# A chunked scan and two mixture layers on one core: the order of the opening, of the weight splits, and of the last columns

## The chip, the cores and the metric

The kernel runs on one core of a Trainium2 chip, in one launch. The metric is the time of one execution on the device in microseconds (us). The core's engines are TensorE (PE in the profile; PEld is its weight load), VectorE (DVE), ScalarE (ACT), GpSimd (POOL) and SyncE (SP), which issues nearly all DMAs.

## The reference

```python
# attention: batch 4, heads 8, seq 768, head_dim 32, state 16
L = np.exp(cum[:, :, :, None] - cum[:, :, None, :]) * causal
M = np.einsum('bhin,bhjn->bhij', Cc, Bc) * L
y = np.einsum('bhij,bhjd->bhid', M, xc) + (C @ state) * np.exp(cum)
state = decay_full * state + sum_j B_j x_j * exp(cum_end - cum_j)
# mixture of 4 experts over 3072 tokens, 256 wide, 1024 hidden
p = domain_probs / (domain_probs.sum(-1, keepdims=True) + 1e-09)
for e in range(E):
    out += p[:, e:e + 1] * (np.maximum(x @ w1[e], 0.0) @ w2[e])
# dense layer, 1536 hidden
return (silu(x @ w_gate) * (x @ w_val)) @ w_out
```

Inputs and output are float32. The chunk length of the scan is the kernel's own choice, as it does not alter what is computed.

## The kernel before

The scan runs in chunks of 128 positions. There are 24 of them, numbered q, 4 batches for each of 6 steps in time. A chunk's y, transposed, is a block of 128 tokens for the first layer. Each 32-bit factor is split into a rounded high part and a low part, and each product of a layer is three products: high by high, low by high, high by low. So weights have to be split too: `w_h` is a copy (ScalarE or POOL), `w_l` a subtraction.

**Opening** (`begin`, line 289, and the code from line 1326). TensorE first runs three products of ones that nothing reads (line 1342), then four mask products (line 198). Once the logarithms of `a` are there (`spaced`, `la`, lines 294 and 295), two prefix products make the cumulated logarithms of chunks 0 and 1 (line 291, `pt` and `py`), VectorE copies them (lines 301 and 302), and 32 small products add them as rows to the masks (`first_rows`, line 205). `first_scores` (line 221) are the products of B and C; ScalarE and VectorE make the decay `L` (lines 239, 248, 253), and `first_weights` (line 257) multiplies scores and decay. `a_heads` (line 546) makes y, `a_done_high` and `a_done_low` (lines 591, 597) split it into `xh` and `xl`, and then the first layer can start. On the way, two products compute the cumulated logarithms of all later chunks and what is left of each chunk (`pc`, lines 308 and 309), two more the rows `crow` that are stored to DRAM (line 334), and read back, spread over the partitions, as `L` of the later chunks (line 419).

**Stream.** From there on the order is written by hand. A unit (e, t, f) is 128 hidden columns f of expert e for token tile t (tiles 0 and 1 have 256 tokens). `m_hidden(u)` (line 662) makes six products into one of three PSUM banks, and ScalarE and VectorE turn them into `hh` and `hl`; `m_out` (line 676) of the unit three before follows. With the last unit of a tile, VectorE multiplies the result by the share of the expert (`tmp`, line 695), and only then may the next tile use the PSUM bank. A unit has two slots; `put(s, fn)` lets `fn` issue its instructions in slot s. What stands in a slot is found in tables: `PAIRS` and `SLOTS` (lines 1370 and 1372) hold the steps of later chunks (per chunk: mask on POOL, exponentials, splits `Cs` and `Bs`, scores; per pair: the slot of its y), and `split_later` (line 1424) the splits of the weights, (e, part), in two pieces each, high and low. `keeps` saves the state after chunks 0 and 1, `blocks_made` makes a block matrix of it on POOL (`bd`), `pair_loads(4)` loads `L` and more for chunks 4 and 5.

**End.** The dense layer uses fewer products by sums of operands. Its last piece, in `plain_product` (line 1254), is made in two halves of 256 columns by `products` (line 990); VectorE adds each half (line 1291), and SP and ScalarE store one each (line 1252).

Of the kernel before, what the change touches and what calls it, by code (L numbers as in the profile page):

```python
# [24 lines left out]
def kernel(ctx: ExitStack, tc: tile.TileContext, nat_d, bc_d, bc0_d, a_d, probs, w1, w2, wg, wv, wo, out):  # L25
# [12 lines left out]
    nc = tc.nc  # L38
    P = 128
# [215 lines left out]
    def first_weights(q, z):  # L255
        L = Q[q]["L"][z]
        nc.vector.tensor_tensor(out=L, in0=first[q][z].rearrange("p (h i) -> p h i", h=4), in1=L, op=ALU.mult)
# [31 lines left out]
    def begin(rows):  # L289

        mm = lambda out, w, v, start=False: nc.tensor.matmul(out, w, v, start=start, stop=True, skip_group_check=True)
        nc.vector.tensor_scalar(out=la, in0=la, scalar1=1e-6, scalar2=1.0, op0=ALU.max, op1=ALU.min)
        n = NFIRST * H
        nc.scalar.activation(out=spaced[:, :, :4], in_=la[:, :n].rearrange("p (g r) -> p g r", r=4), func=AF.Ln)
        nc.scalar.activation(out=la, in_=la, func=AF.Ln)
        nc.scalar.activation(out=wj[:, :1], in_=la[:, :1], func=AF.Exp)
        pt = hidden_bank(512)
        mm(pt[:, :P], spaced.rearrange("p g r -> p (g r)"), upper, True)
        py = ps_s.tile([P, 512], F32, tag="s", name="pc")
        mm(py[:, :n], upper, la[:, :n], True)  # L300
        nc.vector.tensor_copy(sums, pt[:, :P])
        nc.vector.tensor_scalar(out=cum[:, :n], in0=py[:, :n], scalar1=-1.0, scalar2=None, op0=ALU.mult)
        first_rows(rows)
        first_scores(0)
        pr = pt[:GR, P:3 * P]
        for g in range(2):
            mm(pr[:, g * P:(g + 1) * P], la[:, g * GR:(g + 1) * GR], upper)
        mm(py[:, n:NR], upper, la[:, n:])
        mm(py[:, 320:], lower, la)
        high, low = split_parts(0, 0)  # L310
        G = nc.gpsimd
        for z in range(2):
            high(z, G)
            low(z, G)
        first_direct(0, 0, rows[0])
        first_decay(0, 1, rows[1])
        first_decay(1, 0, rows[2])
        first_exp(0, 1)
        first_weights(0, 0)
        first_exp(1, 0)  # L320
        first[1] = out_banks(512)
        first_scores(1)
        mm(pt[:, 3 * P:], ones, ones)
        first_direct(1, 1, rows[3])
        first_weights(0, 1)
        y = ps_y.tile([P, 2, 512], F32, tag="y", name="y01")
        for q in range(2):
            a_place(q, y)
        Q[0]["yv"] = hidden_bank(512)[:, :KD * P].rearrange("p (k i) -> p k i", k=KD)
        Q[0]["y"] = [Q[0]["yv"][:, k, :] for k in range(KD)]  # L330
        a_heads(0, True)
        first_weights(1, 0)
        nc.scalar.activation(out=crow, in_=pr.rearrange("p (g i) -> p g i", g=2), func=AF.Copy)
        nc.sync.dma_start(out=crow_d.rearrange("(g r) i -> r g i", g=2), in_=crow)
        a_load(2)
        expert_load(1, 0, bacc[4])
        a_load_cum(2)
        a_load_nat(2)
        a_load_cum(3)
        a_load_nat(3)  # L340
        first_weights(1, 1)
        a_done_high(0)
        a_done_low(0)
        a_heads(1, True)
        nc.scalar.activation(out=wj, in_=py[:, 320:], func=AF.Exp)
        a_done_high(1)
        a_done_low(1)
        nc.vector.tensor_scalar(out=cum[:, n:], in0=py[:, n:NR], scalar1=-1.0, scalar2=None, op0=ALU.mult)
        high, low = split_parts(0, 1)
        high()  # L350
        for q in range(2):
            a_weigh_b(q, nc.gpsimd)
        low(0, nc.vector)
        return py, lambda: low(1, nc.vector)
# [185 lines left out]
    def a_heads(q, start=False):  # L540
        r = Q[q]
        per = P // D
        for h in range(H):
            j = h % per
            M = r["L"][h // 4][:, h % 4, :] if isinstance(r["L"], list) else r["L"][:, h, :]
            nc.tensor.matmul(  # L546
                r["y"][h // per][j * D:(j + 1) * D, :],
                r["x"][:, h, :],
                M,
                start=(start and h < per),  # L550
                stop=True,
                skip_group_check=True,
            )
# [30 lines left out]
    def a_done_high(q):  # L584
        yv = Q[q]["yv"]
        if q * P >= PLAIN:
            b, o = divmod(q * P, BN)
            nc.scalar.activation(out=bacc[b][:, :, o:o + P], in_=yv, func=AF.Copy)
        else:
            t, o = tile_of(q)  # L590
            nc.scalar.activation(out=xh[t][:, :, o:o + P], in_=yv, func=AF.Copy)
# [395 lines left out]

    retired = []

    def products(ps, w, v, start, stop, parts=1):  # L990
        (wh, wl), (vh, vl) = w, v
        n = BN // parts
        for z in range(0, BN, n):
            for i, (x, y) in enumerate([(wh, vh), (wl, vh), (wh, vl)]):
                nc.tensor.matmul(  # L995
                    ps[:, z:z + n], x, y[:, z:z + n], start=(start and i == 0), stop=(stop and i == 2), skip_group_check=True
                )

    def split(v, engine):
# [250 lines left out]
    def store(src, d, b, z=0, queue=None):  # L1250
        n = src.shape[-1]
        (queue or nc.sync).dma_start(out=out[d * P:(d + 1) * P, b * BN + z:b * BN + z + n], in_=src)

    def plain_product(p, k):

        which, q = divmod(k, NQD)
        tail = p == NPAIR - 1
        V = nc.vector
        fresh = q == 0 and (which != 1 or tail)
        if fresh:  # L1260
            accs[p, which, ""] = bank(*banks[which]) if tail and which else bank(dpools["ps"], "d2")
        elif q == 0:
            accs[p, which, ""] = accs[p, which - 1, ""]
        ps = accs[p, which, ""]
        last = tail and k == 4 * NQD - 1
        parts = 2 if last else 1
        products(ps, wq.pop((p, "plain", k)), sides[p, "plain", k], fresh, q == NQD - 1, parts)
        drop_split(sides.pop((p, "plain", k)))
        if q < NQD - 1:
            return  # L1270
        b1, b2 = 2 * p, 2 * p + 1
        if which == 0:
            c = cs[p] = grab()
            nc.scalar.activation(out=c, in_=ps, func=AF.Copy)
        elif which == 1:
            c = cs[p] if tail else grab()
            if tail:
                chore(9)
                V.tensor_tensor(out=c, in0=ps, in1=c, op=ALU.add)
            else:  # L1280
                nc.scalar.activation(out=c, in_=ps, func=AF.Copy)
            store(c, 1, b1)
            drop(c)
        else:
            if tail:
                chore(9)
            v, d, b = ((ends[p][1], 1, b2), (ends[p][0], 0, b1))[which - 2]
            n = BN // parts
            for i in range(parts):
                f = slice(i * n, (i + 1) * n)  # L1290
                V.tensor_tensor(out=v[:, f], in0=ps[:, f], in1=v[:, f], op=ALU.add)
                store(v[:, f], d, b, i * n, (nc.sync, nc.scalar)[i])
            drop(v)

    order = [(p, k) for p in range(NPAIR) for k in range(4 * NQD)]
# [30 lines left out]
    with tc.manual_schedule():  # L1326
# [11 lines left out]
        constants()  # L1338
        s0 = ps_y.tile([P, 2, 512], F32, tag="y", name="s0")
        first[0] = [s0[:, z] for z in range(2)]  # L1340
        for _ in range(3):
            nc.tensor.matmul(first[0][0][:, :P], ones, ones, start=True, stop=True)
        rows = out_banks(512) + [hidden_bank(512) for _ in range(2)]
        for v in rows:
# [13 lines left out]
        def put(s, *fns):  # L1358
            for fn in fns:
                todo.setdefault(slots[s], []).append(fn)  # L1360
# [5 lines left out]
        def quad(i, j=0, h=0):  # L1366
            return n0 + (i * NQE + j) * 4 + h


        PAIRS = [(0, 0, 28), (0, 0, 46), (0, 0, 60), (6.3, 1.1, 72.5), (6.8, 0.9, 85), (4.3, 1, 95), (4.3, 0.8, 103), (5.8, 1, 117), (5.8, 1.1, 129), (6.8, 1.2, 141), (4.3, 1, 151)]  # L1370

        SLOTS = {
# [6 lines left out]
        }  # L1379

# [57 lines left out]
        put(2, lambda: (mixture(), head_constants()))  # L1438
        put(3, lambda: (mixture_parts(), mixture_store()))
        put(5, lambda: (adds(), loads()))  # L1440
        put(6, keeps)
        put(8, blocks_made)
        put(10, lambda: totals(py[:, 320:]))
        put(14, decays)
        split_later(0, 2, (0, 1), (3, 4))
        split_later(0, 3, (4, 5), (6, 7))
        split_later(1, 0, (6, 9), (10, 13))
        split_later(1, 1, (14, 15), (16, 17), nc.gpsimd)
        split_later(1, 2, (17, 19), (19, 21), nc.gpsimd)
        split_later(1, 3, (26, 27), (28, 29), nc.gpsimd)  # L1450
        put(11, lambda: pair_loads(4))

        seq, t1 = expert_tokens(0, bacc[4], bacc[5])
        for step, slot in zip(seq + [t1], (72, 76, 80, 86, 90, 94, 98, 104), strict=True):
# [304 lines left out]
```

## Time and profile before

| what | value |
|---|---|
| median of 3 runs | 821.24 us (821.04 to 822.31) |
| the profiled execution, own time | 821.02 us |
| its span | 819.3 us |
| PE busy | 811.0 us (99%) |
| DVE, ACT, POOL busy | 563.1, 550.3, 506.2 us |
| DMA | 129.06 MB, mean 158 GB/s |

The span goes from the first to the last instruction that the profiler sees; the time of the execution holds a little more. Busy time is the sum in which an engine has an instruction under way. Where an engine idles, the profile names what ended the idle time: an instruction of another engine, or a DMA. A row of the order of time gives start and duration in us, the engine, the line of the kernel, what is written and read, and how many instructions are merged into the row; in brackets the idle time ahead of it.

### The profile page before, as it was taken

Reading aid. Unit: us, or ns where it says so; the run is one execution under the profiler, and the core shown is the slowest. Engines: PE = TensorE matmul, PEld = TensorE weight load, DVE = VectorE, ACT = ScalarE, POOL = GpSimd, SP = SyncE. Lnnn points to the kernel's source line nnn. Section 1 sums busy time; section 2 is a strip of 40 time slices with the busy share of each in tenths; the row PEclk is TensorE's granted clock in tenths of the full one; section 3 lists DMA queues with packets and bytes.
Section 4 is the critical chain, followed back from the end, with each engine's and each line's share of the span. In section 5 each row is a group of like instructions: output and inputs, shape, how many; then the busy total and the mean of one; then the engine's idle time right before and its main releaser. Section 6 shows DMA issues by size and latency. Waiting matters only on the chain.

```text
span 819.3 us, 12893 instructions
## 1 busy us (share of the span) xinstructions
PE 811.0 (99%) x4361; PEld 671.1 (82%) x4361; DVE 563.1 (69%) x861; ACT 550.3 (67%) x1110; POOL 506.2 (62%) x527
## 2 busy tenths in 40 slices
PE   8999999999999999999999999999999999999998
PEld 7998887888778888888888888887787888888876
DVE  6877567565267855466756565737889878877767
ACT  7687776756476566767766667556577677777763
POOL 5654776434498533777978367313688568847752
PEclk9999999999999999999999999999999999999999
DMA  8864546541302226353552342363556366637651
GB/s 289 281 222 150 162 149 226 172 169 52 116 14 78 90 88 227 97 174 107 164 167 68 121 146 94 138 237 109 174 175 199 129 229 227 227 124 266 228 165 52
DMA packets 67218, 129.06 MB, mean 158 GB/s; under 512 B 6288, under 2 KB 34512, under 8 KB 67152
## 3 DMA queue, kind: packets, MB, share of 16 engines
q1 hardware_dynamic: 67008, 128.11, 47.2%
q8 instruction: 34, 0.56, 0.3%
q14 instruction: 32, 0.26, 0.1%
q10 hardware_dynamic: 144, 0.13, 0.0%
HBM read 108.41 MB, written 19.81 MB: 157 GB/s over the span
## 4 chain that ended last, share of the span: by engine, by line
PE 93%; POOL 2%; ACT 2%; DVE 1%; issue 1%; DMA 1%; DVEq 0%; POOLq 0%; ACTq 0%; SPq 0%
PE h L968 32%; PE d L1088 11%; PE po L1088 10%; PE h L631 10%; PE po L639 9%; PE d L968 7%; PE d L995 6%; PE o L995 3%; PE ypsum L546 1%; PE h L995 1%; PE scores L475 1%; PE ypsum L491 1%; DMA L<-crow_d 1%; POOL acc L872 0%; POOL xl L715 0%
## 5 line engine op out<-in xcount | busy, mean ns | idle before, releaser
L1053 DVE TENSOR_TENSOR d<-d,c 128x512 f32<-128x512 f32 x32 | 22.4, 699 | 103.1 <-ACT c L1050 103.1
L673 DVE SCALAR_TENSOR_TENSOR hl<-h,hh 128x512 fp32r<-128x512 f32 (+1 forms) x80 | 46.5, 582 | 59.7 <-ACT hh L672 59.4
L1088 PE MATMUL d<-hh,we_o 128*128 128x512 f32 x256 | 78.8, 389 | 0.0
L1088 PE MATMUL po<-hh,we_o 128*128 128x512 f32 x256 | 78.8, 389 | 0.0
L1037 DVE SCALAR_TENSOR_TENSOR hl<-h,hh 128x512 fp32r<-128x512 f32 x96 | 65.9, 688 | 17.9 <-PE d L1088 12.9
L672 ACT ACTIVATE hh<-h 128x512 fp32r<-128x512 f32 (+1 forms) x80 | 40.5, 509 | 53.8 <-PE h L631 52.8
L1036 ACT ACTIVATE hh<-h 128x512 fp32r<-128x512 f32 x96 | 57.0, 597 | 26.3 <-DVE h L1057 22.8
L433 ACT ACTIVATE L<-L,cum 128x128 f32<-128x128 f32 x176 | 56.1, 394 | 1.7 <-POOL L L426 1.7
L631 PE MATMUL h<-xh,w_h 128*128 128x512 f32 (+1 forms) x160 | 56.5, 354 | 0.7 <-POOL Bw L461 0.7
L968 PE MATMUL h<-xh,wq_h 128*128 128x512 f32 x144 | 56.5, 392 | 0.4 <-DVE ds L1139 0.3
L639 PE MATMUL po<-hh,w_h 128*128 128x512 f32 (+1 forms) x160 | 56.3, 352 | 0.6 <-DVE tmp L695 0.6
L1088 PEld LDWEIGHTS d<-hh,we_o 128*128 128x128 f32 x256 | 48.1, 188 | 10.0
L1088 PEld LDWEIGHTS po<-hh,we_o 128*128 128x128 f32 x256 | 48.0, 188 | 10.0
L968 PE MATMUL h<-xh,wq_l 128*128 128x512 f32 x144 | 56.1, 390 | 0.0
L968 PE MATMUL h<-xl,wq_h 128*128 128x512 f32 x144 | 56.1, 390 | 0.0
L631 PE MATMUL h<-xh,w_l 128*128 128x512 f32 (+1 forms) x160 | 55.8, 349 | 0.0
L639 PE MATMUL po<-hh,w_l 128*128 128x512 f32 (+1 forms) x160 | 55.6, 347 | 0.0
L639 PE MATMUL po<-hl,w_h 128*128 128x512 f32 (+1 forms) x160 | 55.5, 347 | 0.0
L631 PE MATMUL h<-xl,w_h 128*128 128x512 f32 (+1 forms) x160 | 55.3, 347 | 0.0
L968 PE MATMUL h<-xh,we_h 128*128 128x512 f32 x128 | 50.0, 391 | 0.1
L968 PE MATMUL h<-xl,we_h 128*128 128x512 f32 x128 | 49.8, 389 | 0.0
L968 PE MATMUL h<-xh,we_l 128*128 128x512 f32 x128 | 49.8, 389 | 0.0
(492 smaller groups left out, 2539.4 us busy)
## 6 DMA issues: line engine op xcount, KB each, us to landing
wq_h<-wd_d SPq DMA_DIRECT2D x36, 448.0 KB
wq_l<-wd_d SPq DMA_DIRECT2D x36, 448.0 KB
L<-crow_d SPq DMA_DIRECT2D x22, 512.0 KB
bc<-in_bc_dram SPq DMA_DIRECT2D x21, 512.0 KB
wq_o<-wp_d SPq DMA_DIRECT2D x24, 384.0 KB
raw_q<-in_w_dram SPq DMA_DIRECT2D x32, 256.0 KB
wq_s<-ws_d SPq DMA_DIRECT2D x18, 384.0 KB
pbc<-probs_d SPq DMA_DIRECT2D x22, 256.0 KB
```

The costliest lines, as they stand in the source:

```text
L433: nc.scalar.activation(out=L[:, h, :], in_=L[:, h, :], func=AF.Exp, bias=cols(cum, q)[:, h:h + 1])
L475: nc.tensor.matmul(ps[:, 2 * g:2 * g + 2, :], r["Bs"][:, 2 * half + g, :], r["Cs"][:, 2 * half + g], start=(g == 0), stop=True, skip_group ...
L631: nc.tensor.matmul(ps, w[:, k, fs], v[:, k, :], start=(i == 0), stop=(i == len(ops) - 1))
L639: nc.tensor.matmul(po[d], w[:, fc, dsl], x, start=(first and i == 0), stop=(last and i == 2))
L672: nc.scalar.activation(out=hh, in_=ph, func=AF.Relu)
L673: nc.vector.scalar_tensor_tensor(out=hl, in0=ph, scalar=0.0, in1=hh.bitcast(F32), op0=ALU.max, op1=ALU.subtract)
L968: nc.tensor.matmul(ps, x[:, ws], y, start=(start and i == 0), stop=(i == 2), skip_group_check=True)
L995: nc.tensor.matmul(ps[:, z:z + n], x, y[:, z:z + n], start=(start and i == 0), stop=(stop and i == 2), skip_group_check=True)
L1036: S.activation(out=hh, in_=ps, func=AF.Relu)
L1037: return lambda: V.scalar_tensor_tensor(out=hl, in0=ps, scalar=0.0, in1=hh.bitcast(F32), op0=ALU.max, op1=ALU.subtract)
L1053: V.tensor_tensor(out=W, in0=W, in1=v, op=ALU.add)
L1088: nc.tensor.matmul(po[d], both[:, z, dsl], y, start=(first and i == 0), stop=(last and i == 2), skip_group_check=True)
```

## The change

Of the three products of ones, one stays ahead of the masks and one goes behind the prefix products; the third product of ones, later in `begin`, is dropped. The two products for the later chunks are written behind y of chunk 0. The second half of chunk 1's weights and `xh` of chunk 0 come ahead of `crow`. In the tables, chunk 5's steps come two slots earlier, one step of chunks 2 and 7 moves by a slot, the pair 4 and 5 by one; the pieces of the weight splits are spaced anew, and the high part of expert 1's first weights is made on POOL in place of ScalarE. The last columns are made, added and stored in pieces of 256, 128 and 128.

```diff
@@ begin
         mm(py[:, :n], upper, la[:, :n], True)
+        mm(first[0][0][:, :P], ones, ones, True)
         nc.vector.tensor_copy(sums, pt[:, :P])
...
             mm(pr[:, g * P:(g + 1) * P], la[:, g * GR:(g + 1) * GR], upper)
-        mm(py[:, n:NR], upper, la[:, n:])
-        mm(py[:, 320:], lower, la)
         high, low = split_parts(0, 0)
...
         first_scores(1)
-        mm(pt[:, 3 * P:], ones, ones)
         first_direct(1, 1, rows[3])
...
         a_heads(0, True)
+        mm(py[:, n:NR], upper, la[:, n:])
+        mm(py[:, 320:], lower, la)
         first_weights(1, 0)
+        first_weights(1, 1)
+        a_done_high(0)
         nc.scalar.activation(out=crow, in_=pr.rearrange("p (g i) -> p g i", g=2), func=AF.Copy)
...
         a_load_nat(3)
-        first_weights(1, 1)
-        a_done_high(0)
         a_done_low(0)
@@ products
-    def products(ps, w, v, start, stop, parts=1):
+    def products(ps, w, v, start, stop, edges=(0, BN)):
         (wh, wl), (vh, vl) = w, v
-        n = BN // parts
-        for z in range(0, BN, n):
+        for z, end in zip(edges, edges[1:]):
             for i, (x, y) in enumerate([(wh, vh), (wl, vh), (wh, vl)]):
                 nc.tensor.matmul(
-                    ps[:, z:z + n], x, y[:, z:z + n], start=(start and i == 0), stop=(stop and i == 2), skip_group_check=True
+                    ps[:, z:end], x, y[:, z:end], start=(start and i == 0), stop=(stop and i == 2), skip_group_check=True
                 )
@@ plain_product
-        parts = 2 if last else 1
-        products(ps, wq.pop((p, "plain", k)), sides[p, "plain", k], fresh, q == NQD - 1, parts)
+        edges = (0, BN // 2, 3 * BN // 4, BN) if last else (0, BN)
+        products(ps, wq.pop((p, "plain", k)), sides[p, "plain", k], fresh, q == NQD - 1, edges)
...
-            n = BN // parts
-            for i in range(parts):
-                f = slice(i * n, (i + 1) * n)
+            for i, (z, end) in enumerate(zip(edges, edges[1:])):
+                f = slice(z, end)
                 V.tensor_tensor(out=v[:, f], in0=ps[:, f], in1=v[:, f], op=ALU.add)
-                store(v[:, f], d, b, i * n, (nc.sync, nc.scalar)[i])
+                store(v[:, f], d, b, z, (nc.sync, nc.scalar)[i % 2])
@@ the opening and the tables
-        for _ in range(3):
+        for _ in range(1):
             nc.tensor.matmul(first[0][0][:, :P], ones, ones, start=True, stop=True)
...
-        PAIRS = [(0, 0, 28), (0, 0, 46), (0, 0, 60),
+        PAIRS = [(0, 0, 28), (0, 0, 47), (0, 0, 60),
...
-            5: (31, 33, 34, 34, 36, 40, 45),
+            5: (29, 31, 32, 32, 36, 38, 43),
             6: (37, 39, 40, 42, 43, 47, 50),
-            7: (44, 46, 47, 48, 50, 54, 57),
-            2: (8, 10, 11, 12, 13, 14, 10),
+            7: (44, 46, 46, 48, 50, 54, 57),
+            2: (8, 10, 11, 12, 14, 14, 10),
...
-        put(6, keeps)
+        put(7, keeps)
...
-        split_later(0, 2, (0, 1), (3, 4))
+        split_later(0, 2, (1, 2), (1, 2))
         split_later(0, 3, (4, 5), (6, 7))
-        split_later(1, 0, (6, 9), (10, 13))
-        split_later(1, 1, (14, 15), (16, 17), nc.gpsimd)
+        split_later(1, 0, (6, 9), (10, 13), nc.gpsimd)
+        split_later(1, 1, (13, 15), (15, 16), nc.gpsimd)
...
-        put(11, lambda: pair_loads(4))
+        put(10, lambda: pair_loads(4))
```

Three places show what moves. The first is TensorE in the opening, from the products for the rows `crow` (`upper,la`) to y of chunk 1; `s`, `po` and `h` are PSUM tiles, `pc` is `py`. Before:

```order
L291 MATMUL h_179<-upper,la 96x128 x2
L291 MATMUL pc<-la,upper 128x176
L291 MATMUL pc<-la,lower 128x192
L221 MATMUL po_228<-acc_88 128x128
...
L221 MATMUL po_229<-acc_88 128x128
L291 MATMUL h_179<-ones 128x128
L546 MATMUL h_245<-L,nat 32x128 x8
L546 MATMUL y_244<-L,nat 32x128 x8
```

With the change:

```order
L291 MATMUL h_177<-upper,la 96x128 x2
L221 MATMUL po_225<-acc_88 128x128
...
L221 MATMUL po_226<-acc_88 128x128
L546 MATMUL h_241<-L,nat 32x128 x8
L291 MATMUL pc<-la,upper 128x176
L291 MATMUL pc<-la,lower 128x192
L546 MATMUL y_240<-L,nat 32x128 x8
```

The scores of chunk 1 and y of chunk 0 (line 546, first row) now come right behind the `crow` products, and the `pc` products lie between the two chunks' y; the product of ones is gone.

The second is POOL early in the stream, from the shares `pn` to the first `Bw` of a later chunk. `acc_90` and `acc_91` hold the raw weights of expert 1, parts 0 and 1; line 271 is the high part, line 426 the mask of a chunk. Before:

```order
L370 TENSOR_TENSOR pn<-pin,psm 128x96
L426 AFFINE_SELECT L<-L 128x1024
L577 TENSOR_TENSOR bd<-pairblk,st 128x128 x2
L426 AFFINE_SELECT L<-L 128x1024
L461 TENSOR_TENSOR Bw<-nat,wj 128x128
L271 CAST w_1_0_h<-acc_91 128x512 x2
```

With the change:

```order
L370 TENSOR_TENSOR pn<-pin,psm 128x96
L271 CAST w_1_0_h<-acc_90 128x512
L426 AFFINE_SELECT L<-L 128x1024
L577 TENSOR_TENSOR bd<-pairblk,st 128x128 x2
L271 CAST w_1_0_h<-acc_90 128x512
L426 AFFINE_SELECT L<-L 128x1024
L271 CAST w_1_0_h<-acc_91 128x512
L461 TENSOR_TENSOR Bw<-nat,wj 128x128
```

Two casts are new on this queue, one ahead of the first mask and one behind the blocks.

The third is VectorE at the end of tile 0, where `tmp` (line 695) frees the PSUM bank; the numbers tell the `h` banks apart. Before:

```order
L673 SCALAR_TENSOR_TENSOR hl<-h_791,hh 128x256
L453 SCALAR_TENSOR_TENSOR Cs<-bc,csel,Cs 128x4x128 x2
L484 TENSOR_TENSOR L<-scores,L 128x512
L673 SCALAR_TENSOR_TENSOR hl<-h_821,hh 128x256
L695 TENSOR_TENSOR tmp<-po_609,pbc 128x256
```

With the change:

```order
L453 SCALAR_TENSOR_TENSOR Cs<-bc,csel,Cs 128x4x128 x2
L673 SCALAR_TENSOR_TENSOR hl<-h_798,hh 128x256
L484 TENSOR_TENSOR L<-scores,L 128x512
L673 SCALAR_TENSOR_TENSOR hl<-h_819,hh 128x256
L695 TENSOR_TENSOR tmp<-po_607,pbc 128x256
```

The two `Cs` pieces of chunk 5 now stand ahead of one more `hl`, so one unit earlier.

## Rows read from the trace of the kernel before

**Rows 1.** The page: busy us, share and count of TensorE; granted clock in 40 slices.
```profile
PE 811.0 (99%) x4361; PEld 671.1 (82%) x4361; DVE 563.1 (69%) x861; ACT 550.3 (67%) x1110; POOL 506.2 (62%) x527
PEclk9999999999999999999999999999999999999999
```

**Rows 2.** Waits of TensorE: for whom, us in total, times, longest.
```profile
PE h L631 <- POOL Bw L461: 0.7, 1, 0.7
PE po L639 <- DVE tmp L695: 0.6, 1, 0.6
```

**Rows 3.** Order of time, TensorE, the opening: start, duration, instruction, idle time before.
```profile
1.10 1.65 PE L1342 MATMUL s<-ones 128*128 128x128 f32 x6 [1.10 <-DVE ones L127]
2.54 1.06 PE L198 MATMUL po<-above,upto 128*128 128x512 bf16 x2
...
4.25 0.56 PE L291 MATMUL h<-upper,spaced 128*128 128x128 f32 x2
...
5.29 0.38 PE L205 MATMUL po<-sums,pick 32*128 32x128 f32 x2 [0.35 <-DVE cum L302]
...
7.79 0.46 PE L291 MATMUL pc<-la,upper 128*128 128x176 f32 x2
...
8.51 1.16 PE L221 MATMUL po<-acc 16*128 16x128 f32 x16
9.60 0.49 PE L291 MATMUL h<-ones 128*128 128x128 f32 x2
10.01 0.64 PE L546 MATMUL h<-L,nat 128*32 128x128 f32 x16
...
11.11 0.43 PE L546 MATMUL y<-L,nat 128*32 128x128 f32 x8 [0.17 <-DVE L L257]
12.21 0.36 PE L631 MATMUL h<-xh,w_h 128*128 128x256 f32 x1 [0.67 <-POOL Bw L461]
```

**Rows 4.** Order of time, ScalarE, the opening.
```profile
3.12 0.22 ACT L294 ACTIVATE spaced<-la 128x16 f32<-128x16 f32 x1 [1.05 <-DVE la L292]
...
8.51 1.16 ACT L253 ACTIVATE L<-h,cum 128x128 f32<-128x128 f32 x4
10.12 0.38 ACT L333 ACTIVATE crow<-h 96x256 f32<-96x256 f32 x1 [0.45 <-PE h L291]
```

**Rows 5.** Order of time, VectorE, the opening and the end of tile 0.
```profile
7.70 1.28 DVE L257 TENSOR_TENSOR L<-s,L 128x512 f32<-128x512 f32 x2
9.77 1.29 DVE L257 TENSOR_TENSOR L<-po,L 128x512 f32<-128x512 f32 x2 [0.79 <-PE po L221]
...
41.34 1.41 DVE L453 SCALAR_TENSOR_TENSOR Cs<-bc,csel,Cs 128x512 fp32r<-128x512 f32 x2
...
43.60 0.75 DVE L695 TENSOR_TENSOR tmp<-po,pbc 128x256 f32<-128x256 f32 x2
```

**Rows 6.** Order of time, POOL, from the opening to 26 us.
```profile
9.38 1.28 POOL L275 TENSOR_TENSOR w_l<-raw,w_h 128x512 fp32r<-128x512 f32 x1
...
18.15 1.63 POOL L426 TENSOR_SCALAR_AFFINE_SELECT L<-L 128x1024 f32<-128x1024 f32 x1 [1.76 <-DMA L<-crow_d]
19.75 0.88 POOL L577 TENSOR_TENSOR bd<-pairblk,st 128x128 f32<-128x128 f32 x2
...
23.10 2.54 POOL L271 CAST w_h<-acc 128x512 fp32r<-128x512 f32 x4 [0.35 <-DMA acc<-in_w_dram]
```

**Rows 7.** Order of time, TensorE and its weight load, in the stream.
```profile
17.08 0.19 PEld L631 LDWEIGHTS h<-xh,w_l 128*128 128x128 f32 x1 [0.23 <-DVE w_l L275]
...
23.73 0.28 PE L631 MATMUL h<-xh,w_h 128*128 128x256 f32 x1
...
44.16 0.36 PE L639 MATMUL po<-hh,w_h 128*128 128x256 f32 x1 [0.55 <-DVE tmp L695]
```

**Rows 8.** Order of time, the last products and adds.
```profile
814.67 0.87 PE L995 MATMUL d<-t24l,wq_o 128*128 128x256 f32 x6
815.58 0.76 DVE L1291 TENSOR_TENSOR acc<-d,acc 128x256 f32<-128x256 f32 x2 [0.70 <-PE d L995]
```

More of the change, by code (lines that the diff above doesn't have):

```diff
@@ L1367, in quad @@
             return n0 + (i * NQE + j) * 4 + h
-        PAIRS = [(0, 0, 28), (0, 0, 46), (0, 0, 60), (6.3, 1.1, 72.5), (6.8, 0.9, 85), (4.3, 1, 95), (4.3, 0.8, 103), (5.8, 1, 117), (5.8, 1.1, 129), (6.8, 1.2, 141), (4.3, 1, 151)]
+        PAIRS = [(0, 0, 28), (0, 0, 47), (0, 0, 60), (6.3, 1.1, 72.5), (6.8, 0.9, 85), (4.3, 1, 95), (4.3, 0.8, 103), (5.8, 1, 117), (5.8, 1.1, 129), (6.8, 1.2, 141), (4.3, 1, 151)]
         SLOTS = {
             4: (22, 24, 25, 26, 28, 29, 35),
[1 row of a table removed]
[1 row of a table added]
             6: (37, 39, 40, 42, 43, 47, 50),
[2 rows of a table removed]
[2 rows of a table added]
             3: (13, 15, 16, 17, 18, 22, 22),
```

## The prediction

> **What bounds the kernel now.** I read the page first, then the waits of TensorE, then its order of time in three stretches, and last the order of time of the other engines just ahead of each wait. The page shows TensorE busy for 811.0 of 819.3 us [rows 1], so there are 8.3 us in which it does not work, and only changes to those, or to products that it need not do in their place, can move the end. The waits of TensorE [rows 2] name the two longest that this change is near: 0.7 us ahead of the first product of the first layer, put down to Bw, and 0.6 us on tmp. The third thing to see is that "busy" hides something in the opening: up to 12.21 us [rows 3] TensorE does small products whose only purpose is to let the first layer start, so their order counts, busy or not. From 12.21 us on the products follow each other closely, and what the stream gains at its start it keeps, unless some other engine or a DMA cannot follow.
>
> Times are against the profiled execution: span 819.3, its own time 821.02, which is 0.22 under the median of the three runs, 821.24.
>
> **Fillers ahead.** Three of them run from 1.10 to the masks at 2.54, so 0.48 each [rows 3]. The four masks take 1.71 (2.54 to 4.25), 0.43 for 512 columns, which is the 1.2 GHz level. With two fillers gone the masks could end at 3.29 instead of 4.25, but the prefix product behind them loads spaced, which ScalarE writes from 3.12 to 3.34 [rows 4], and the load of it (an estimate of 0.2 or 0.3, from the 0.40 that the product's two passes take) comes first. I take 3.6, so 0.65 earlier. **Filler behind.** TensorE idles 0.35 ahead of the row products at 5.29 [rows 3]; the filler lies in that hole, moved to 4.29 to 4.64. At 0.48 it sticks out by 0.13, at the higher clock by nothing. The row products therefore start 0.6 earlier, with 0.3 (spaced's load slower, filler all cold) and 0.75 as the ends.
>
> **Order behind the row products.** Two things leave the path of the first chunk's y: the later totals' products (7.79 to 8.51, 0.72) and the last product of ones (9.60 to 10.01, 0.41) [rows 3]. That last one also writes the PSUM tile from which ScalarE copies crow, and crow starts at 10.12, behind it [rows 4], with xh of the first chunk queued behind crow. In the new order:
> - scores of chunk 1 start at 8.51 - 0.72 - 0.6 = 7.19 and take 1.09, to 8.28;
> - VectorE's weights of chunk 0 end at 8.98 [rows 5], now 8.38, so y of chunk 0 starts at 8.4 instead of 10.01 and ends near 8.9;
> - the totals' 0.72 follow, to about 9.65, beside VectorE's weights of chunk 1, which cover them;
> - those weights have two releasers. Half 0 needs the scores (8.28) and VectorE free (8.38): 8.4 to 9.0. Half 1 needs ScalarE's direct exponentials, which end at 8.51 + 1.16 = 9.67 [rows 4], now 9.07: with half of the 1.29 [rows 5] it ends at 9.75;
> - the second half of chunk 1's y starts 0.05 behind that, as before (11.06 and 11.11): 9.8. That is 1.3 earlier.
>
> From there to the first layer it is y, ScalarE's xh, the first load: 12.21 - 1.3 = 10.9. Crow, wj and xh of chunk 0 fit on ScalarE before that, since crow no longer waits for the ones. If the totals' products were late, wj would be late and with it Bw on POOL; but nothing in the stream reads Bw for three units. POOL's low half of the first weights ends at 9.38 + 1.28 = 10.66 [rows 6] and does not move with any of this; the fourth product of the layer reads it, some 0.4 behind the first. So the gain here is 1.3, with 0.7 (no gain from the fillers at all) and 1.45 as ends, and POOL would stop it soon after.
>
> **Respaced splits.** The low half of the weights of part 2 holds TensorE at 17.08 for 0.23 [rows 7]. Its VectorE pieces move from slots 3 and 4 to 1 and 2, ahead of one hl and of the reciprocal, and ScalarE's copies alternate with hh: I take 0.2, and hl and the reciprocal that now stand behind them have over a unit to spare. **Chunk 5's steps** move two slots earlier. At 44.16 TensorE waits 0.55 for tmp [rows 7]; VectorE starts tmp at 43.60 with no idle time ahead of it [rows 5], so it was late through its own queue, in which the two Cs pieces (1.41 from 41.34) stand a few instructions ahead. With these gone from there tmp starts when the products allow, and hl of the unit before is then the last thing ahead of it: 0.5, with 0.3 and 0.55 as ends. Pair 4 and 5 a slot later, keeps a slot later and the L loads a slot earlier cost nothing that I can find: y of that pair is read from slot 64 on, the blocks of keeps first in that pair, and SP issues its DMAs in the same order as before, with one store more at the end.
>
> **POOL gets two casts** of expert 1's first weights, from ScalarE: about 0.64 each by the 2.54 for four [rows 6]. The first falls in the 1.76 idle ahead of the mask at 18.15 and costs nothing; the second stands behind that mask and the blocks. That is the weak place, see the third rival.
>
> **Last columns.** VectorE's first add starts at 815.58, when all six products have ended (814.67 + 0.87 = 815.54), not the first three [rows 8]; its order shows one wait for all pieces, before and after. So three pieces do not let the adds start earlier. The products become three of 256 and six of 128 columns: 0 to 0.36 longer (half the time each, or the same); I take 0.1, near the lower end, since 16 score products of 128 columns take 1.09. The adds take 0.1 more than the 0.76. Against that the last piece to be stored is 64 KB and not 128. Its store is issued some 0.2 later, on SP, behind SP's first, and moves in less: 0, between a loss and a gain of 0.2.
>
> **Sum:** 1.3 + 0.2 + 0.5 + 0 = 2.0, so 819.0 for such an execution and 819.2 for the median.
>
> **The clock.** The masks run at the 1.2 GHz level and the last products, six of 256 columns in 0.87, at 2.4 [rows 3, 8], while the page's granted clock shows 9 in every slice [rows 1]: the change of level is too early for it. TensorE was working from 1.10 until then almost without a hole. The new order keeps that: one filler, masks, prefix, a filler, rows. The Trainium skill (TensorE: Matmul & The Clock Gate, What's actually happening) says that the throttled state is the default and that activity releases it; by that rule fewer fillers speak against this change, and it is the second rival. The trace agrees that the opening starts low; no row here shows a hole that delays the release.
>
> **Rivals.**
> 1. *The stream starts earlier, but waits later for what DMAs bring.* POOL waits for DMAs at 18.15 and at 23.10 [rows 6]; those landings hardly move, since crow, which starts the first of them, is a copy of only 0.8 earlier and its queue is full. Behind 23.10 stand four casts (2.54), VectorE's low halves, and hl in VectorE's order. For: these copies are now a slot or two earlier in VectorE's queue, so hl waits behind them. Against: hl lags its reader by three units. If it takes 1.2 of the 1.3: 820.4. Chance 0.22.
> 2. *The clock rises later.* Products between 5.29 and 8.0 (2.7 us) would take twice that. The gain of 1.3 turns into a loss of 1.4; the other terms (0.7) stay: 821.9. Chance 0.08.
> 3. *Slower: the second cast on POOL.* The layer's first unit of expert 1 starts at 23.73 [rows 7], at 22.2 in the new order, and its second half reads the low piece about 0.5 later, 22.7. On POOL that cast is queued behind the mask (1.63), which waits for L's DMA, and the blocks (0.88) [rows 6]: with the landing at 18.15 the cast ends at 21.3, and VectorE's low piece near 22. It decides from a landing of 18.9 on, and each us more is one us of wait. Slower than now by over 0.2% needs a landing at about 22.5: 823 and more. Against: crow is issued earlier, not later. Chance 0.05.
> 4. *The change does not do what it says in the opening:* spaced or the filler gives the two fillers' time back. Then 0.7 + 0.2 + 0.5 (ends as above): 819.8. Chance 0.10.
>
> **How the numbers follow.** Forecast 0.55: 819.2, by its ends 818.6 to 819.7. 0.2% of 821.24 is 1.64, about what a measurement of this kernel can tell from no change, so faster means under 819.6, slower over 822.9. Nearly all of the forecast (0.53), a third of rival 4 and a little of rival 1 are faster: 0.58. Rival 3 and the tail of rival 2 are slower: 0.06. The rest is 0.36. The range reaches up to rival 1 and past it a little, 820.9, and down to 818.4, where all terms are at their good ends.
>
> **What would show it.** Right: first product of the layer near 10.9 (12.21 before); y of chunk 0 ahead of the totals' products, near 8.4; no waits at the places of 17.08 and 44.16; first mask near 1.6 to 1.75; TensorE's idle time near 7; the last add still behind the last product. Wrong: the first row product later than 5.0, a new wait of TensorE on w_l or hl between 20 and 35 us, or a first layer at 10.9 with the same end, which would put the loss behind 45 us, where I see no cause.

## The result, and the profile after

The changed kernel takes **825.82 us** (median of 6, 823.95 to 826.33) against 821.17 for the kernel before (6 runs, 821.04 to 822.34): a ratio of 1.0051, 95% interval 1.0041 to 1.0061. It is slower by 4.65 us where 2.0 of gain were forecast. The profiled execution took 826.33, with a span of 824.6, 5.3 more than before.

The page first, busy time and granted clock, as in [rows 1]:

```profile
PE 817.5 (99%) x4360; PEld 676.5 (82%) x4360; DVE 567.5 (69%) x862; ACT 549.2 (67%) x1108; POOL 506.9 (61%) x529
PEclk9999999999999999999999999999999999999999
```

TensorE has one instruction less and is busy 6.5 us longer. So the time did not go into a wait. Its waits, as in [rows 2], say the same:

```profile
PE h L631 <- ACT xh L591: 0.7, 1, 0.7
PE ypsum L546 <- ACT L L433: 0.3, 1, 0.3
PE po L639 <- ACT ec L468: 0.2, 1, 0.2
```

The 0.6 on tmp is gone. The wait of the first layer is as long as before and now put down to xh. The order of time on TensorE shows where the 5.3 us are (start, duration, instruction, idle time before; compare [rows 3]):

```profile
1.10 0.80 PE L1340 MATMUL s<-ones 128*128 128x128 f32 x2 [1.10 <-DVE ones L127]
1.72 1.03 PE L198 MATMUL po<-above,upto 128*128 128x512 bf16 x2
...
3.49 0.77 PE L291 MATMUL h<-upper,spaced 128*128 128x128 f32 x2
4.05 0.45 PE L291 MATMUL pc<-la,upper 128*128 128x16 f32 x2
4.34 0.77 PE L291 MATMUL s<-ones 128*128 128x128 f32 x2
5.04 0.58 PE L205 MATMUL po<-sums,pick 32*128 32x128 f32 x2
...
6.91 1.92 PE L221 MATMUL s<-acc 16*128 16x128 f32 x16
8.76 1.17 PE L291 MATMUL h<-upper,la 128*96 128x128 f32 x4
9.86 2.08 PE L221 MATMUL po<-acc 16*128 16x128 f32 x16
11.86 1.08 PE L546 MATMUL h<-L,nat 128*32 128x128 f32 x16
...
16.16 0.55 PE L631 MATMUL h<-xh,w_h 128*128 128x256 f32 x1 [0.67 <-ACT xh L591]
...
19.71 0.41 PE L631 MATMUL h<-xh,w_l 128*128 128x256 f32 x1
19.92 0.41 PE L631 MATMUL h<-xl,w_h 128*128 128x256 f32 x1
...
21.18 0.28 PE L631 MATMUL h<-xh,w_l 128*128 128x256 f32 x1
21.30 0.28 PE L631 MATMUL h<-xl,w_h 128*128 128x256 f32 x1
```

The row products start at 5.04, 0.25 before [rows 3]. From there on the same products take 1.7 to 1.8 times as long: 16 score products 2.08 instead of 1.16, 16 products of y 1.08 instead of 0.64. The products of the first layer, 256 columns, start 0.21 apart at 19.71 and 0.12 apart at 21.18. So TensorE leaves the 1.2 GHz level at about **21.1 us**; the trace's clock record has the change at 21.09, and at 4.61 in the kernel before. TensorE was at work without a hole from 1.10 to beyond 15 us. The page's clock row shows 9 in the first slice of 20.6 us all the same: the trace's record has no entry ahead of this change, and that time is shown as full clock. So the level of so short a stretch is to be read from the spacing of the products.

The first layer starts 3.95 later than before, and by the end of the stretch at the low level the stream is 6.1 behind. At the places of the respaced splits and of chunk 5's steps it wins back 0.3 and 0.4 (5.8 behind, then 5.4). Most of the other 0.4 comes past 700 us: there the kernel before waits 0.3 for `ds` (line 1139), and the changed kernel does not. The end, as in [rows 8]:

```profile
819.72 1.14 PE L994 MATMUL d<-t24l,wq_o 128*128 128x256 f32 x9
820.89 0.82 DVE L1289 TENSOR_TENSOR acc<-d,acc 128x256 f32<-128x256 f32 x3 [0.96 <-PE d L994]
```

The last group starts 5.05 later than in [rows 8], and the span ends 5.3 later: the tail costs 0.25.

### The profile page after: what moved, and what is told of

It reads as the page before. It is cut to its first block, busy times and chain, and to the rows that moved or that the text cites. A ratio compares the mean times of both kernels' runs of the same rounds, so it can differ in the third digit from the quotient of the medians.

```text
span 824.6 us, 12898 instructions
## 1 busy us (share of the span) xinstructions
PE 817.5 (99%) x4360; PEld 676.5 (82%) x4360; DVE 567.5 (69%) x862; ACT 549.2 (67%) x1108; POOL 506.9 (61%) x529
## 4 chain that ended last, share of the span: by engine, by line
PE 93%; POOL 2%; ACT 2%; DMA 1%; issue 1%; DVE 0%; SPq 0%; DVEq 0%; POOLq 0%; ACTq 0%
PE h L968 32%; PE d L1087 11%; PE po L1087 10%; PE h L631 9%; PE po L639 8%; PE d L968 7%; PE d L994 6%; PE o L994 3%; DMA L<-crow_d 1%; PE h L994 1%; PE ypsum L546 1%; PE scores L475 1%; PE ypsum L491 1%; POOL acc L872 0%; POOL xl L715 0%
## 5 line engine op out<-in xcount | busy, mean ns | idle before, releaser
L1087 PE MATMUL d<-hl,we_o 128*128 128x512 f32 x128 | 49.8, 389 | 0.0
```

Of the source, the lines that this page charges most:

```text
L1087: nc.tensor.matmul(po[d], both[:, z, dsl], y, start=(first and i == 0), stop=(last and i == 2), skip_group_check=True)
```

## The experiments

**Theory A:** the loss is the later rise of TensorE's clock, and the two products of ones taken from the start are what brought it about. **Rivals:** the new order of the opening loses time of itself; the tables make new waits in the stream. The first four kernels take the change apart. In the diffs, "ahead" is the loop of products of ones in front of the masks, "behind" the one after the prefix product. The kernel before has three ahead, none behind and one more later in `begin`, so four in all; the changed kernel has two.

**1. The changed kernel, three ahead.**

```diff
-        for _ in range(1):
+        for _ in range(3):
             nc.tensor.matmul(first[0][0][:, :P], ones, ones, start=True, stop=True)
```

> The changed kernel with three products of ones ahead of the masks again, and the one behind the prefix products kept. Clock theory (the two products taken away ahead of the masks leave TensorE at its 1.2 GHz level until 21 us): the level rises before 6 us as in the kernel before, the first product of the first layer comes near 11.3, and the time is 819 to 820.5. Order theory (the new order behind the row products costs the time by itself, the low level only goes with it): the first layer stays behind 15 us and the time over 823.

Measured: 820.67 (819.32 to 822.43, 11 runs), ratio 0.9992 (0.9982 to 1.0001). The clock rises at 5.23, the first layer starts at 11.88 (11.3 was expected), and the loss is gone, with a median just over the expected range. All the rest of the change is in this kernel, so the rest is not the loss.

**2. The kernel before, with the fillers of the change alone.**

```diff
         mm(py[:, :n], upper, la[:, :n], True)
+        mm(first[0][0][:, :P], ones, ones, True)
...
-        for _ in range(3):
+        for _ in range(1):
```

> The kernel before with one edit of the change alone: one product of ones ahead of the masks in place of three, and one behind the prefix products. Clock theory: the products of the first layer start at 0.21 us spacing and the time is 825 to 828, 4 to 7 over the kernel before. Order theory: the time is 820.5 to 821.5.

Measured: 826.07, but in **two groups**: 819.77, 820.3, 820.38 and 820.75, and seven from 826.04 to 826.89; nothing between. Ratio 1.0038 (1.0016 to 1.006). The profiled execution was one of the lower group, 820.3. Its opening:

```profile
1.10 0.80 PE L1343 MATMUL s<-ones 128*128 128x128 f32 x2 [1.10 <-DVE ones L127]
1.72 1.03 PE L198 MATMUL po<-above,upto 128*128 128x512 bf16 x2
...
4.22 0.77 PE L291 MATMUL s<-ones 128*128 128x128 f32 x2
...
8.23 1.16 PE L221 MATMUL po<-acc 16*128 16x128 f32 x16
...
11.94 0.36 PE L632 MATMUL h<-xh,w_h 128*128 128x256 f32 x1 [0.67 <-POOL Bw L462]
12.13 0.28 PE L632 MATMUL h<-xh,w_l 128*128 128x256 f32 x1
12.25 0.28 PE L632 MATMUL h<-xh,w_h 128*128 128x256 f32 x1
```

Here the clock rose at 5.15. So the fillers alone bring the loss, but not in each execution.

**3. The kernel before, with the tables alone** (chunk steps, pairs, keeps, splits, L loads).

```diff
-            5: (31, 33, 34, 34, 36, 40, 45),
+            5: (29, 31, 32, 32, 36, 38, 43),
...
-        split_later(0, 2, (0, 1), (3, 4))
+        split_later(0, 2, (1, 2), (1, 2))
```

> The kernel before with the tables of the change alone (chunk steps, respaced splits, casts on POOL, keeps and loads by a slot). By the prediction's terms 0.2 and 0.5: no wait at 17.08, most of that at 44.16 gone, time 820.3 to 820.7. If the waits are only replaced by others behind them: 821.0 to 821.4.

Measured: 821.21 (820.38 to 822.55, 11 runs), ratio 1.0000 (0.9991 to 1.0008). In its profile, the waits of TensorE:

```profile
PE h L631 <- POOL Bw L461: 0.7, 1, 0.7
PE ypsum L546 <- ACT L L433: 0.4, 1, 0.4
PE po L205 <- DVE cum L302: 0.2, 1, 0.2
PE po L639 <- ACT ec L468: 0.2, 1, 0.2
```

The 0.6 on tmp is gone, and so is the wait at 17.08. From the first product of the first layer to the end of the span it takes 806.38, against 807.09 before: 0.71 less. The median lies where the rival (waits only replaced) was expected, but it can't settle this, at an interval of some 0.7 us to either side; the gain is read from one profile.

**4. The kernel before, with the order of the opening alone** (three ahead, none behind).

```diff
-        mm(py[:, n:NR], upper, la[:, n:])
-        mm(py[:, 320:], lower, la)
...
-        mm(pt[:, 3 * P:], ones, ones)
...
         a_heads(0, True)
+        mm(py[:, n:NR], upper, la[:, n:])
+        mm(py[:, 320:], lower, la)
...
```

> The kernel before with the order of the change behind the row products alone (totals' products between the two chunks' y, second weights and xh ahead of crow, last product of ones dropped), three products of ones ahead as before. By the prediction's working without its filler term: the first layer starts 0.7 us earlier, near 11.5, and the time is 820.3 to 820.7. If the order itself costs, as by the order theory: over 822.

Measured: 820.73 (819.81 to 822.34, 11 runs), ratio 0.9994 (0.9985 to 1.0002); first layer at 11.89. Its opening behind the row products:

```profile
7.48 0.68 PE L291 MATMUL h<-upper,la 128*96 128x128 f32 x4
8.09 1.16 PE L221 MATMUL po<-acc 16*128 16x128 f32 x16
9.18 0.65 PE L545 MATMUL h<-L,nat 128*32 128x128 f32 x16
9.76 0.56 PE L291 MATMUL pc<-la,upper 128*128 128x176 f32 x2
10.16 0.49 PE L291 MATMUL pc<-la,lower 128*128 128x192 f32 x2
10.57 0.65 PE L545 MATMUL y<-L,nat 128*32 128x128 f32 x16
```

y of chunk 1 (10.57) starts when the totals' products end, with no idle time ahead of it. The rivals fall: neither the order nor the tables lose time.

The next four ask how many products of ones it takes, and where.

**5. The changed kernel, two ahead, one behind** (`range(2)` in the loop ahead).

> The changed kernel with two products of ones ahead of the masks where it has one; the one behind the prefix product stays. Theory A (what costs the time is that TensorE goes from 1.2 to 2.4 GHz at 21.09 us and not near 5 us, and what decides is how much TensorE works ahead of about 5 us): with one of the two fillers given back part of the executions, or all, have the early rise; those lie at 819.5 to 822.5, the others near 826, and nothing lies between 823 and 825. Theory B (all three fillers ahead are needed): all executions near 825.8. Theory C (the later rise is an accident of one execution and the lost time lies in the order): near 825.8 too, but with an early rise in the profile.

Measured: 820.85 (819.11 to 822.12), all 11 below 823; ratio 0.9992 (0.9983 to 1.0). One more filler is enough in these executions; theories B and C fall.

**6. The changed kernel, one ahead, three behind.**

```diff
-        mm(first[0][0][:, :P], ones, ones, True)
+        for _ in range(3):
+            mm(first[0][0][:, :P], ones, ones, True)
```

> The changed kernel with one product of ones ahead of the masks, and three instead of one behind the prefix product: as many as in the run with three ahead, two of them 2 us later. The row products then start near 6.0 us (5.04 in the changed kernel, 0.48 for each of two more). Theory A (the amount of work ahead of about 5 us decides, not where it stands): the two more come only between 4.3 and 5.8 us; if that still counts, all executions lie at 820 to 823, with the rise near 6; if it does not, most near 826.5, with the rise near 21. Theory B (the place counts, an unbroken start from 1.10 us): near 826.5 in all.

Measured: 821.52 (819.19 to 826.24, 12 runs), nine of them at most 822.41 and three at 824.84, 826.15 and 826.24; ratio 1.0011 (0.9995 to 1.0028). So fillers that come only at 4.3 us still make the early rise more frequent (nine of 12; without a filler behind two of 12, in run 7; with one behind nine of 30, by the table below), but not sure. The profiled execution, 819.19, has the earliest rise of all, 4.37, and the row products at 5.18 and not near 6.0:

```profile
4.32 0.93 PE L291 MATMUL s<-ones 128*128 128x128 f32 x6
5.18 0.38 PE L205 MATMUL po<-sums,pick 32*128 32x128 f32 x2
...
8.86 0.64 PE L547 MATMUL h<-L,nat 128*32 128x128 f32 x16
...
11.57 0.36 PE L632 MATMUL h<-xh,w_h 128*128 128x256 f32 x1 [0.67 <-ACT xh L592]
```

**7. The changed kernel, one ahead, none behind.**

```diff
-        mm(first[0][0][:, :P], ones, ones, True)
```

> The changed kernel without the product of ones behind the prefix product, and with one ahead. Theory A (the amount of TensorE's work in the opening decides when 2.4 GHz comes): even fewer executions with the early rise than in the changed kernel, so none of 11: all at 824 to 827, rise near 21 us in the profile. Rival (the filler behind is what delays the rise, by holding up the row products): the early rise comes back, 820 to 822.

Measured: 825.2 (819.61 to 826.14, 12 runs); two at 819.61 and 820.1, ten from 823.89 up; ratio 1.0036 (1.0021 to 1.0051). The profile (826.14) has the rise at 21.19. "None of 11" was too strict. Two of 12 and nine of 30 are too few to tell one filler behind from none; but the filler behind is not what delays the rise.

**8. Three ahead, none behind, two pieces at the end** (the rest as changed).

> A version meant to beat both: the changed kernel with three products of ones ahead as before the change and none behind, and with the kernel before's last columns in two pieces. By the terms read so far: early rise in all executions, the order of the opening 0.3 to 0.4 us, the slots of the splits 0.7, no loss of 0.25 in the tail: 820.2 in the median against 821.2, lowest near 819.2. If the order and the slots do not add up, 820.7.

Measured: 820.94 (820.26 to 821.86, 11 runs), ratio 0.9993 (0.9984 to 1.0001): 0.7 more than expected, though all lie below 823. The profiled execution, 821.86, has the rise at 6.59 and a wait that the profiles of runs 1 to 7 do not have. TensorE, POOL, ScalarE and VectorE, one after the other:

```profile
25.65 0.39 PE L630 MATMUL h<-xh,w_l 128*128 128x256 f32 x1 [1.21 <-DVE w_l L275]
```

```profile
21.50 1.10 POOL L425 TENSOR_SCALAR_AFFINE_SELECT L<-L 128x1024 f32<-128x1024 f32 x1 [3.27 <-DVE w_l L275]
...
23.39 0.61 POOL L271 CAST w_h<-acc 128x512 fp32r<-128x512 f32 x1
```

```profile
22.64 1.28 ACT L432 ACTIVATE L<-L,cum 128x128 f32<-128x128 f32 x4 [3.37 <-POOL L L425]
23.83 0.36 ACT L671 ACTIVATE hh<-h 128x256 fp32r<-128x256 f32 x1
```

```profile
24.22 0.42 DVE L672 SCALAR_TENSOR_TENSOR hl<-h,hh 128x256 fp32r<-128x256 f32 x1 [2.78 <-ACT hh L671]
24.56 1.03 DVE L275 TENSOR_TENSOR w_l<-acc,w_h 128x512 fp32r<-128x512 f32 x1
```

The mask starts at 21.50 instead of 18.15 [rows 6], and TensorE waits 1.21 for VectorE's low piece (24.56). That is the late mask of the third rival, but its second cast is not the last link: it ends at 24.00. What holds the low piece until 24.56 is hl ahead of it in VectorE's queue; hl waits for ScalarE's hh, and hh stands behind exponentials that wait for the mask. The mask itself waits for L: VectorE's w_l, which the row names, is no input of it, and in run 11, with the same wait, the row names L's DMA. That load is issued at 13.77 in run 11 and at 14.05 in run 5, whose mask starts at 18.19; why it lands later isn't known, nor how many of the executions have this wait.

**9. The changed kernel again**, unaltered.

> The changed kernel, unaltered, in more executions. Theory A (the rise of TensorE's clock comes by chance early or late, and the less TensorE does before 5 us the rarer it is early): most of the executions at 824 to 827, with at most 4 of 11 at 819 to 822. Rival (the changed kernel always has the late rise): all at 823.9 to 826.5.

Measured: 824.45 (818.84 to 826.03, 12 runs), ratio 1.0019 (0.9999 to 1.0038). Five lie at 818.84, 818.96, 819.69, 821.12 and 821.78, seven from 823.93 to 826.03. So the changed kernel has the early rise too, in some executions; one more than the bound of four that was set. The profiled one (825.23) rises at 20.26.

**10. The kernel of run 2 again**, for a second profile.

> The kernel before with only the fillers moved, unaltered, for a second profile. Theory A: if this execution takes about 826, its clock rises near 21 us and its first layer starts near 16; if it takes about 820, the rise is near 5 us and the first layer near 11.9, as in the first profile. Rival (the two groups differ in something other than the clock, a DMA for one): a time of 826 with a first layer near 12 and the loss later.

Measured: 826.52, rise at 20.85. Its opening, line for line beside that of run 2:

```profile
1.10 0.79 PE L1343 MATMUL s<-ones 128*128 128x128 f32 x2 [1.10 <-DVE ones L127]
1.72 1.03 PE L198 MATMUL po<-above,upto 128*128 128x512 bf16 x2
...
4.17 0.77 PE L291 MATMUL s<-ones 128*128 128x128 f32 x2
...
10.91 2.08 PE L221 MATMUL po<-acc 16*128 16x128 f32 x16
...
16.25 0.55 PE L632 MATMUL h<-xh,w_h 128*128 128x256 f32 x1 [0.67 <-POOL Bw L462]
16.60 0.42 PE L632 MATMUL h<-xh,w_l 128*128 128x256 f32 x1
16.82 0.41 PE L632 MATMUL h<-xh,w_h 128*128 128x256 f32 x1
```

The same program, and the same 16 products between 1.10 and 5.00 us, starts within 0.06 us of each other, busy 3.90 of 3.90 us in both. In one execution the level rises at 5.15, in the other at 20.85, and the first layer starts 4.31 apart. When run 10's level rises, its stream is 6.3 behind; at the end it is 6.2. So the difference in time is the clock's, and it isn't set by the program alone. The two profiles come from different chips, but run 2's eleven executions, all on one chip, fall into both groups, and so do run 9's; so the chip alone does not set it either.

**11. Two ahead, one behind, two pieces at the end** (the rest as changed).

> The changed kernel with two products of ones ahead and one behind, and the kernel before's last columns in two pieces: early rise in all executions, 0.25 less in the tail than with two ahead and three pieces (820.85): 820.6 in the median, lowest near 819. Rival (the pieces cost nothing): 820.85.

Measured: **819.77** (818.82 to 821.73, 11 runs), ratio **0.9984** (0.9975 to 0.9992). It is the only version whose interval lies wholly below the kernel before, by 0.7 to 2.1 us. It is 0.8 lower than expected and 1.1 below run 5, of which the tail explains 0.25; the rest is open. Its profiled execution, 821.08, one of the two longest, has the rise at 7.29 and again 1.2 on w_l, with the mask at 21.43, as in run 8.

All executions of these kernels, by the fillers:

| ahead, behind | kernels | below 823 us | above |
|---|---|---|---|
| 3, 0 or 1 | before (98 runs), 1, 3, 4, 8 | 142 | 0 |
| 2, 1 | 5, 11 | 22 | 0 |
| 1, 3 | 6 | 9 | 3 |
| 1, 1 | changed, 2, 9, 10 | 9 | 21 |
| 1, 0 | 7 | 2 | 10 |

## Why the prediction was wrong

**The step that failed is the paragraph on the clock,** with the fillers' gain that rests on it. It took the rise as unmoved because "The new order keeps that: one filler, masks, prefix, a filler, rows", with TensorE at work nearly without a hole. The order did keep it: between 1.10 and 5.04 there is no hole in the changed kernel. But working without a hole is not enough: runs 2 and 10 work alike up to 5 us and rise 15.7 us apart. The rule of the Trainium skill that was set against the change (TensorE: Matmul & The Clock Gate, What's actually happening: the low level is the default, activity releases it) had the direction right, as the table shows. The same section of the Trainium skill says that the moment varies from run to run of one kernel, and gives half a microsecond to either side. The runs agree that it varies, but by far more: 5.15 and 20.85 for the one kernel of runs 2 and 10. One profile of the kernel before, with one rise, could not show that the fillers made an early rise sure.

**Rival 2 was the case that came,** with its price wrong: it took the low level to last from 5.29 to 8.0, so 821.9. It lasted to 21.09, and the first layer's products lie in it: 825.8. Its chance, 0.08, was too small: the fillers are products without a use, and the prediction had found no other reason for them in the rows.

**The other terms,** read where the clock rises early:

- *Fillers, 0.6 (ends 0.3 and 0.75):* 0.25 in the changed kernel, 0.36 in run 2 (rows at 4.93). The masks (1.72) and the product of spaced (3.49, forecast 3.6) came as forecast. The filler behind was mis-sized: it takes 0.70 (4.34 to 5.04), not 0.48. Without it the rows start at 4.71 (run 7), so it sticks out by 0.33 and not by 0.13. The first row product, at 5.04, is past the 5.0 that the prediction named as a sign of being wrong.
- *Order, 0.7:* about 0.5. From the row products to the first layer it is 6.92 in [rows 3] and 6.39 in runs 1 and 6. The step that failed is "beside VectorE's weights of chunk 1, which cover them". In run 6 those weights end at 10.32 (9.03 + 1.29), but the totals' products, the last thing ahead of y of chunk 1, hold all of it until 10.26. Its second half, which the forecast has 0.05 behind the weights, starts at 10.50, 0.18 behind them: 0.13 lost. The weights end about 0.1 later, from the start of the row products, than forecast, which is the rest. So the first layer came at 11.57 at best, not at 10.9.
- *Splits and chunk 5's steps, 0.2 + 0.5:* 0.3 and 0.4 at their places in the profiles of runs 1 and 3 and of the changed kernel. Right; at the second, a wait of 0.2 on ec is what comes next. The 0.71 of run 3's whole profile adds two things that the prediction does not have: by 212 us 0.25 is lost again, and past 700 us the wait of 0.3 on `ds` is gone, as in all profiles with the new tables and in none without. Why isn't known.
- *POOL's casts, 0:* right in the changed kernel. In the profiles of runs 8 and 11 the late mask of rival 3 costs 1.2, by way of ScalarE's exponentials and hl and not of the cast; it is the new wait on w_l between 20 and 35 us that the prediction named as a sign.
- *Tail, 0 (ends 0.2 to either side):* 0.25 lost. From the start of the last products to the end of the span it is 4.63 before and 4.62 to 4.64 in runs 2 to 4, and 4.88 and 4.87 in the changed kernel and run 1. The last add stays behind the last product, as forecast; nine products take 1.14 where six take 0.87, so 0.27 and not 0.1.

With an early rise these are 0.25 + 0.5 + 0.7 - 0.25 = 1.2, so 820.0 by the median of the kernel before. Run 9's five lie around that, 818.84 to 821.78, with 819.69 in the middle.

## What to carry to other kernels

Products without a use ahead of the real work may be there to make TensorE's clock rise early in every execution, and not only in some: before one takes them out, one should price the whole stretch at the low level and look at more than one execution, since a single profile shows one rise. Cut such fillers one at a time and look at the spread of the times, not at the median alone: here two ahead instead of three lost nothing, and one ahead and one behind lost about 5 us in two of three executions. What is left of a change with a loss in it is found by putting back one part: with two fillers ahead and the old tail the same change is faster.

## What was not expected of the hardware

The same program takes 819.77 or 826.89 (run 2), with the same work on TensorE up to 5 us, by when the level rises: in the profiles at 4.37 to 7.29, or at 20.26 to 21.19. Some times (823.89 to 825.05) lie below those of all the profiles with a late rise (825.23 to 826.52), so the rise may have other places; none of those was profiled. What of the fillers counts, their number, their time or what they read, was not tried. The early rise itself moves the time: with the order of the changed kernel the first layer comes 6.39 behind the row products where the rise is at 4.37, and 7.34 where it is at 7.29 (run 11: 5.25 and 12.59). That is 1 us; the runs of the kernel before differ by 2.7, and whether this is part of it isn't known, as there is one profile.
